# Fused sliding-window attention and leaky-ReLU MLP on one core: the first values loaded as bf16 into their blocks, shared reciprocals, and a new order of the opening

## The chip, the cores and the metric

The kernel runs on one core of a Trainium2 chip. That core has a matrix engine (TensorE, "PE" in the profile; its weight loads are "PEld"), a vector engine (VectorE, "DVE"), a scalar engine (ScalarE, "ACT"), GpSimd ("POOL") and SyncE ("SP"), which here only starts transfers. Each works through its own queue in order. Sixteen DMA engines move data between main memory and on-chip memory; their work comes from SP's queue (plain copies and DMA transposes) and from POOL's queue (copies that also cast fp32 to bf16).

The metric is the device time of one execution in microseconds. Before the change it is 320.06 us, the median of three runs (319.31 to 320.48).

## The reference

Eight batches of eight heads, 576 tokens, head size 64; attention within a window of 32 tokens to either side; then a two-layer MLP over the heads side by side (4608 tokens of 512 values, 2048 hidden).

```python
scores = scale * np.matmul(q, k.transpose(0, 1, 3, 2))
mask = np.abs(pos[:, None] - pos[None, :]) <= 32
scores = np.where(mask, scores, -1000000000.0)
attn = np.exp(scores - max) / (sum + 1e-09)
x = np.matmul(attn, v)            # then heads side by side: 4608 x 512
h = x @ w_in                      # 512 x 2048
g = np.maximum(0.01 * h, h)
out = g @ w_out                   # 2048 x 512
```

All inputs and the output are fp32 in main memory; the kernel computes its matmuls in bf16 with fp32 sums.

## The kernel before, in words

**Tiling.** Two heads make a pair (p = 0..3), and half a batch (288 tokens) is a half. A step of attention is one pair of one half; there are 8 steps to a batch and 64 in all, numbered i = 8·batch + 4·half + pair. Keys and values of a pair lie in block-diagonal tiles (`kbd`, `vbd`, 128x128 blocks of 64 tokens with head a in partitions and columns 64a..64a+63), so that one matmul serves both heads; the off-diagonal parts are zeroed once. A step runs as follows; the letters are those of the opening's list.

- S: five score matmuls into the PSUM tile `ps` (line 322).
- X: the exponential on ACT (line 331). M: the product with the 0/1 window mask on DVE or POOL (line 336), into `prob`.
- B: the sums of each token's exponentials by matmul with `ones_bd`, a 128x128 block of ones for each head, so that each sum comes out in all 64 partitions of its head (lines 363 and 366). R: the reciprocal of these sums on DVE, 128x288 in fp32 (line 374).
- P: five matmuls of `prob` with `vbd` into a PSUM tile (line 396). U: that product times the reciprocal, on DVE, into the bf16 activations `xT` (line 410).

**The MLP.** For each half g there are sixteen H tiles (128 hidden features by 288 tokens, four matmuls over the four pairs, line 424), each followed by E, the leaky ReLU on ACT into `gT` (line 431). An output tile ("o tile") is 128 tokens by 512 and sums sixteen matmuls over the hidden features (line 454), copied out on ACT (line 459) and stored. H tile of half g needs all four steps of half g; the matmul of chunk c needs pair c alone.

**PSUM.** There are eight banks: four turn in the ring `mm` (H tiles, o tiles, transposes, and the sums and products of a few early steps), two hold `ps`, one is `s` (sums) and one is `x` (products).

**The order.** Everything is placed by hand. The first part of the program, batch 0's attention with the first H tiles, is the list `OPENING`: names with the engine that does them. Besides the letters above, zk/zv clear blocks of `kbd`/`vbd`, cq/ck cast q/k of a pair to bf16, tq/tk transpose them on PE, eq and kA/kB copy them from PSUM into place, cv casts one head's values into `vbd`, wi/wo start one quarter of `w_in`/`w_out` (cast by DMA from POOL, 1 MB read and 512 KB written each), f clears the second set of blocks, and `gate` starts the loads of batch 1, which are held back by a one-element memset of the first tile. After the opening a loop runs H tiles 4 to 15 of half 1 and puts the transposes of batch 1's first two pairs between them (`second_pair`). Then a plan of H and o tiles runs: `spend` is called before each group of four o matmuls and each H tile, adds up a planned time, and runs the steps whose due times have passed. There are sixteen such calls (counted from 0 here) in the four o tiles 0 to 3 that lie between half 1's and half 2's H tiles. Steps 8 to 11, half 2, are due at calls 4, 7, 10 and 12; the third and fourth pair of batch 1 are transposed in calls 0 and 3. From batch 2 on q and k are transposed by DMA after casts on POOL, and the later steps follow due times computed from the plan.

**Loads.** q, k and v of batch 0 are loaded in fp32 by SP, except k of pairs 1 to 3, which a DMA from POOL casts (`load_early`, lines 123 to 134). v is loaded one head at a time, 64 tokens by 9 blocks of 64 values (pieces of 256 bytes), and cast into `vbd` by cv on ACT and POOL.

Of the kernel before, what the change touches and what calls it, by code (L numbers as in the profile page):

```python
# [17 lines left out]
    "zk2:ACT zv2:DVE zk3:ACT win:POOL zv1:DVE cq0:DVE zv0:POOL winc:ACT tq0:PE ck0:DVE eq0:ACT mask0:DVE",  # L18
    "zv3:POOL tk0:PE cq1:DVE kA0:ACT tk1:PE mask1:POOL kB0:ACT tq1:PE kA1:DVE S0:PE cq2:ACT eq1:DVE",
    "tk2:PE X0:ACT kB1:DVE cq3:POOL tq2:PE kA2:ACT M0:DVE S1:PE eq2:ACT kB2:DVE B0:PE X1:ACT tq3:PE",  # L20
    "R0:DVE cv00:POOL S2:PE M1:POOL eq3:ACT tk3:PE X2:ACT cv01:POOL kA3:ACT B1:PE M2:DVE wi0:POOL kB3:ACT",
    "P0:PE R1:DVE B2:PE cv11:ACT wi1:POOL S3:PE cv20:ACT cv10:POOL U0:DVE X3:ACT cv21:POOL P1:PE R2:DVE",
    "cv30:ACT S4:PE M3:POOL P2:PE fill4:PE X4:ACT cv31:ACT S5:PE fill3:PE wi2:POOL U2:DVE B3:PE X5:ACT",
    "U1:DVE wi3:POOL P3:PE R3:DVE S7:PE M5:POOL H0c0:PE H0c1:PE H0c2:PE wo0:POOL X7:ACT U3:DVE B5:PE",
    "M4:DVE H0c3:PE f7:POOL R5:DVE P4:PE E0_0:ACT S6:PE E0_1:ACT wo1:POOL P5:PE E0_3:ACT H0_4:PE E0_2:ACT",
    "gate:POOL wo2:POOL E0_4:ACT H0_5:PE U5:DVE X6:ACT B4:PE M7:DVE wo3:POOL H0_6:PE E0_5:ACT R4:DVE",
    "M6:POOL H0_7:PE E0_6:ACT H0_8:PE E0_7:ACT H0_9:PE E0_8:ACT f3:POOL H0_10:PE E0_9:ACT U4:DVE B6:PE",
    "E0_10:ACT f2:POOL P6:PE R6:DVE H0_11:PE H0_12:PE E0_11:ACT f4:POOL H0_13:PE E0_12:ACT H0_14:PE",
    "E0_13:ACT U6:DVE f0:POOL B7:PE E0_14:ACT H0_15:PE R7:DVE f1:POOL P7:PE E0_15:ACT H1c0:PE f6:POOL",
    "H1c1:PE U7:DVE H1c2:PE f5:POOL H1c3:PE",  # L30
]

SPARE_SUMS, SPARE_PRODUCTS = (0, 1, 2), (0, 1, 5)
# [3 lines left out]
def kernel(  # L37
# [14 lines left out]
    nc = tc.nc  # L52
# [35 lines left out]
    def load_qk(b, p, behind=None):  # L88
# [3 lines left out]
        for into, src, name in ((qf, q, "qf"), (kf, k, "kf")):  # L92
            t = fload.tile([96, 2, RUN * D], FP32, name=f"{name}{p}")
            if behind is not None:
                behind.memset(t[0:1, 0, 0:1], 0.0)
                behind = None
# [25 lines left out]

    def load_early():

        for into, src, name, p in ((qf, q, "qf", 0), (kf, k, "kf", 0), (qf, q, "qf", 1), (qf, q, "qf", 2), (qf, q, "qf", 3)):
            t = fload.tile([96, 2, RUN * D], FP32, name=f"{name}{p}")
            nc.sync.dma_start(out=t, in_=src[0, 2 * p:2 * p + 2].rearrange("a (p c) d -> p a (c d)", c=RUN))
            into[0, p] = t
        for p in range(1, NPAIR):
            t = kb[:, p].rearrange("p c a d -> p (c a d)").rearrange("p (a c d) -> p a c d", c=RUN, d=D)  # L130
            nc.gpsimd.dma_start(out=t, in_=k[0, 2 * p:2 * p + 2].rearrange("a (p c) d -> p a c d", c=RUN))
            early[p] = t
        for p in range(NPAIR):
            load_v(0, p)
# [12 lines left out]


# [205 lines left out]
    def sum_mms(i, spare=False):  # L354

        b, hf, p = where(i)
        pr, both, *_ = probs[i]
        if spare:
            s = mmps.tile([128, 512], FP32, name="mm", tag="mm")[:, 0:HALF]
        else:  # L360
            s = xps.tile([128, HALF], FP32, name="s")
        if both is not None:
            nc.tensor.matmul(s, ones_bd, both, start=True, stop=True)  # L363
        else:
            for n in range(2):
                nc.tensor.matmul(
                    s, ones_bd, pr[:, n].rearrange("p c i -> p (c i)"),
# [334 lines left out]
```

## Time and profile before

| what | value |
|---|---|
| three runs | 320.48, 320.06, 319.31 us |
| the profiled execution's own time | 322.44 us |
| its span, first to last instruction | 320.7 us |
| busy PE / DVE / POOL / ACT | 303.8 / 221.3 / 188.2 / 180.7 us |
| reciprocals (line 374), tile from `s` | 61, 1955 ns each |
| first matmul of half 2's H tiles (line 424) | at 63.50 us |

The profile's page shows one execution: busy time by engine, the span in 40 slices, the chain of work that ended last, and groups of like instructions with the mean of one and with what ended the idle time before them. Two more views are used: the timeline of instructions (start, duration, engine, line, output and inputs, count; in brackets the idle time before and what ended it) and the table of windows (busy time per engine in a stretch, then granted clock, DMA share and GB/s). GB/s counts written bytes, so a casting DMA counts half of what it reads.

### The profile page before, as it was taken

How to read it: one execution, taken by the hardware profiler on the slowest of the kernel's cores; microseconds unless marked ns; L12 is line 12 of the kernel's file. 1: busy time of each engine (PE TensorE's matmuls, PEld its weight loads, DVE VectorE, ACT ScalarE, POOL GpSimd, SP SyncE). 2: the span in 40 equal slices, each digit the busy share in tenths (PEclk: the TensorE clock that was granted, in tenths of full speed). 3: DMA queues.
4: the chain of work that ended last, by engine and by line, in shares of the span. 5: the costliest groups of instructions: out<-in, count | busy, mean ns of one | idle time of the engine just before them, and what ended most of it. 6: DMA issues, size and time to landing. Idle time of an engine off the chain costs nothing.

```text
span 320.7 us, 6477 instructions
## 1 busy us (share of the span) xinstructions
PE 303.8 (95%) x2453; PEld 203.6 (63%) x2453; DVE 221.3 (69%) x264; ACT 180.7 (56%) x391; POOL 188.2 (59%) x247
## 2 busy tenths in 40 slices
PE   1889999999999989999999999999999999999995
PEld 0567764585856747676665857676665857576653
DVE  7879556779656969588845988588845988565100
ACT  6866688383734726465552837465552837464531
POOL 8599764965466856486637866586637866330000
PEclk9999999999999999999999999999999999999999
DMA  8989999996999999399834998399833450010101
GB/s 192 192 141 224 268 240 192 250 187 144 219 255 171 255 192 191 73 223 206 186 76 98 214 231 179 73 190 237 187 76 103 106 72 33 34 38 0 65 35 66
DMA packets 108400, 49.01 MB, mean 153 GB/s; under 512 B 68816, under 2 KB 103888, under 8 KB 108368
## 3 DMA queue, kind: packets, MB, share of 16 engines
q1 hardware_dynamic: 103520, 43.96, 65.3%
q0 software_dynamic: 4848, 4.64, 8.9%
q8 instruction: 19, 0.31, 0.4%
q14 instruction: 13, 0.11, 0.1%
HBM read 36.70 MB, written 9.44 MB: 144 GB/s over the span
## 4 chain that ended last, share of the span: by engine, by line
PE 72%; DMA 12%; POOL 8%; DVE 4%; issue 3%; SPq 1%; ACT 1%; DVEq 0%; POOLq 0%; ACTq 0%
PE mm L454 32%; PE mm L424 31%; DMA vf<-in_v_dram 5%; DMA qf<-in_q_dram 5%; PE x L396 4%; PE ps L322 3%; POOL prob L336 2%; DVE r L374 2%; DMA kT<-kb 2%; PE s L363 2%; POOL kb L221 1%; POOL qb L221 1%; DVE kbd L307 1%; POOL w_in_bf L512 1%; POOL vbd L230 1%
## 5 line engine op out<-in xcount | busy, mean ns | idle before, releaser
L374 DVE RECIPROCAL r<-s 128x288 f32<-128x288 f32 x61 | 119.3, 1955 | 54.7 <-PE s L363 51.6
L424 PE MATMUL mm<-xT,w_in_bf 128*128 128x288 bf16 x1024 | 134.0, 286 | 0.6 <-DVE xT L410 0.4
L454 PE MATMUL mm<-w_out_bf,gT 128*128 128x512 bf16 (+2 forms) x592 | 130.4, 374 | 1.1 <-DMA w_out_bf<-in_moe_w_out_dram 1.1
L336 POOL TENSOR_TENSOR prob<-e,mask 128x576 bf16<-128x576 bf16 x60 | 76.4, 1274 | 88.6 <-issue 42.9
L431 ACT ACTIVATE gT<-mm 128x288 bf16<-128x288 f32 x256 | 101.3, 411 | 28.7 <-PE mm L424 12.3
L424 PEld LDWEIGHTS <-w_in_bf 128*128 128x128 bf16 x1024 | 98.2, 98 | 25.5 <-issue 1.2
L454 PEld LDWEIGHTS <-gT 128*128 128x128 bf16 x592 | 56.2, 98 | 60.5 <-issue 1.2
L459 ACT ACTIVATE o_sb<-mm 128x512 f32<-128x512 f32 (+2 forms) x37 | 21.7, 585 | 92.0 <-PE mm L454 92.0
L331 ACT ACTIVATE e<-ps 128x576 bf16<-128x576 f32 x64 | 41.4, 648 | 9.9 <-PE ps L322 8.3
L230 POOL CAST vbd<-vf 64x576 bf16<-64x576 f32 x52 | 36.2, 696 | 1.6
L307 DVE COPY kbd<-kT 64x576 bf16<-64x576 bf16 x48 | 33.2, 691 | 3.2 <-DMA kT<-kb 2.7
L221 POOL CAST kb<-kf 96x384 bf16<-96x384 f32 (+1 forms) x52 | 31.0, 619 | 5.7 <-DMA kf<-in_k_dram 5.7
L410 DVE TENSOR_TENSOR xT<-x,r 128x288 bf16<-128x288 f32 x61 | 27.9, 458 | 7.9 <-PE x L466 1.7
L322 PE MATMUL ps<-qT,kbd 128*128 128x128 bf16 (+2 forms) x320 | 27.3, 219 | 0.0
L322 PEld LDWEIGHTS <-kbd 128*128 128x128 bf16 x320 | 21.5, 102 | 8.5
L396 PE MATMUL x<-prob,vbd 128*128 128x64 bf16 (+1 forms) x305 | 24.8, 213 | 1.5 <-DVE xT L410 0.9
L396 PEld LDWEIGHTS <-vbd 128*128 128x128 bf16 x320 | 20.8, 99 | 8.0 <-issue 3.7
L221 POOL CAST qb<-qf 96x384 bf16<-96x384 f32 x48 | 24.4, 536 | 0.0
L351 DVE TENSOR_TENSOR both<-prob 128x288 bf16<-128x288 bf16 x52 | 20.7, 398 | 1.0 <-POOL prob L336 0.2
L363 PE MATMUL s<-both,ones_bd 128*128 128x288 bf16 x52 | 14.9, 286 | 1.5 <-DVE r L374 1.5
L251 PE MATMUL tp<-ident,qb 96*128 96x96 bf16 x48 | 4.3, 242 | 5.0 <-DVE qb L258 4.9
L228 ACT ACTIVATE vbd<-vf 64x576 bf16<-64x576 f32 x12 | 8.2, 680 | 0.9 <-DMA vf<-in_v_dram 0.6
(60 smaller groups left out, 95.3 us busy)
## 6 DMA issues: line engine op xcount, KB each, us to landing
qf<-in_q_dram SPq DMA_DIRECT2D x32, 288.0 KB, 4.7
vf<-in_v_dram SPq DMA_DIRECT2D x64, 144.0 KB, 4.3
out_dram<-o_sb SPq DMA_DIRECT2D x35, 256.0 KB, 4.0
kf<-in_k_dram SPq DMA_DIRECT2D x29, 288.0 KB, 4.9
w_in_bf<-in_moe_w_in_dram POOLq DMA_DIRECT2D x4, 512.0 KB, 7.8
w_out_bf<-in_moe_w_out_dram POOLq DMA_DIRECT2D x4, 512.0 KB, 17.5
kb<-in_k_dram POOLq DMA_DIRECT2D x3, 144.0 KB, 8.2
qT<-qb SPq DMA_TRANSPOSE x24, 4.1
```

Of the source, the lines that this page charges most:

```text
L221: eng.tensor_copy(out=to, in_=tok)
L230: eng.tensor_copy(out=vbd[b % 2][r, p, :, r], in_=vf[b, p][r])
L307: nc.vector.tensor_copy(out=to.rearrange("p n (m c) -> p n c m", c=2), in_=kT[r].rearrange("p (c n m) -> p n c m", c=2, n=NB),)
L322: nc.tensor.matmul(ps_v[:, n_, :, i0:i0 + n], kbd[b % 2][:, p, blk], by_c[:, :, hf * EVEN + i0:hf * EVEN + i0 + n], start=True, stop=True,)
L331: nc.scalar.activation(out=es[i], in_=ps[:, P0:P0 + 2 * HALF], func=AF.Exp, scale=scale)
L336: eng.tensor_mul(pr.rearrange("p n c i -> p (n c i)"), es.pop(i), mask[hf].rearrange("p n c i -> p (n c i)"),)
L374: nc.vector.reciprocal(r, probs[i][2])
L396: nc.tensor.matmul(x_v[:, :, i0:i0 + n], vbd[b % 2][:, p, blk, :], pr[:, n_, :, i0:i0 + n], start=(blk == parts[0][1]), stop=(blk == parts ...
L410: nc.vector.tensor_mul(place(i), x, r)
L424: nc.tensor.matmul(h[:, 0:HALF], w_in_bf[:, c, ts(f, 128)], xT[:, c, ds(g * HALF % RING, HALF)], start=(c == 0), stop=(c == DMC - 1),)
L431: nc.scalar.activation(out=gT[:, f, ds(g * HALF % RING, HALF)].rearrange("p (i c) -> p i c", c=2), in_=h[:, 0:HALF].rearrange("p (c i) -> ...
L454: nc.tensor.matmul(o[:, lo:hi], gT[:, f, ds(128 * j % RING, 128)], w_out_bf[:, f, lo:hi], start=(f == 0), stop=(f == FFC - 1),)
```

## The change

1. Batch 0's values come as eight DMAs from POOL (`iv0` to `iv7`, one per head) that cast to bf16 and write straight into `vbd`, in pieces of 128 bytes. The eight fp32 loads on SP and the eight casts (cv) are gone. q of pair 3 also comes by a casting DMA from POOL.
2. Steps 0 and 1, and steps 2 and 3, share one reciprocal. B of these steps uses `gather`, which puts each head's sums of a step into 16 rows (two groups of rows per step) of one PSUM tile; one R serves both steps; G, an fp32 matmul with `spread`, spreads a step's reciprocals to 128 partitions in PSUM; C first copies the product of P into fp32 on-chip memory, and U multiplies the two.
3. Only q and k of batch 1's pair 0 are loaded at `gate`, which moves to DVE. The other pairs and all of batch 1's values are loaded after H tile 6 of half 1, held by a one-element activation on ACT.
4. The opening has a new order and new engines for many items; PE starts with 38 filler matmuls (128 columns) and has 11 more between its first transposes, in place of the seven of 224 columns at steps 4 and 5.
5. After the opening: pair 0 of batch 1 is transposed after H tile 10 and the other three in calls 5, 7 and 9 of the o tiles; sums of step 8 and 9 are made ahead in calls 1 and 8; steps 8 to 11 are due at calls 11, 12, 14 and 15.

```diff
 OPENING = [
-    "zk2:ACT zv2:DVE zk3:ACT win:POOL zv1:DVE cq0:DVE zv0:POOL winc:ACT tq0:PE ck0:DVE eq0:ACT mask0:DVE",
-    "zv3:POOL tk0:PE cq1:DVE kA0:ACT tk1:PE mask1:POOL kB0:ACT tq1:PE kA1:DVE S0:PE cq2:ACT eq1:DVE",
-    "tk2:PE X0:ACT kB1:DVE cq3:POOL tq2:PE kA2:ACT M0:DVE S1:PE eq2:ACT kB2:DVE B0:PE X1:ACT tq3:PE",
-    "R0:DVE cv00:POOL S2:PE M1:POOL eq3:ACT tk3:PE X2:ACT cv01:POOL kA3:ACT B1:PE M2:DVE wi0:POOL kB3:ACT",
-    "P0:PE R1:DVE B2:PE cv11:ACT wi1:POOL S3:PE cv20:ACT cv10:POOL U0:DVE X3:ACT cv21:POOL P1:PE R2:DVE",
-    "cv30:ACT S4:PE M3:POOL P2:PE fill4:PE X4:ACT cv31:ACT S5:PE fill3:PE wi2:POOL U2:DVE B3:PE X5:ACT",
-    "U1:DVE wi3:POOL P3:PE R3:DVE S7:PE M5:POOL H0c0:PE H0c1:PE H0c2:PE wo0:POOL X7:ACT U3:DVE B5:PE",
...
+    "fill38:PE zv2:ACT win:POOL zv1:DVE sel:DVE zk3:ACT ld:POOL winc:DVE zv0:DVE cq0:ACT mask0:DVE",
+    "iv0:POOL tq0:PE fill3:PE zk2:DVE ck0:ACT eq0:DVE iv1:POOL tk0:PE fill8:PE zv3:DVE kA0:ACT iv2:POOL",
+    "cq1:DVE kB0:ACT tk1:PE mask1:DVE iv3:POOL tq1:PE kA1:ACT S0:PE cq2:DVE tk2:PE iv4:POOL kB1:ACT",
+    "eq1:DVE tq2:PE iv5:POOL X0:ACT tq3:PE kA2:DVE S1:PE M0:POOL eq2:DVE kB2:ACT tk3:PE X1:ACT eq3:DVE",
+    "iv6:POOL B0:PE kA3:ACT M1:DVE P0:PE S2:PE kB3:ACT iv7:POOL B1:PE C0:DVE R0:DVE X2:ACT wi0:POOL P1:PE",
+    "S3:PE C1:ACT M2:POOL X3:ACT G1:PE M3:DVE wi1:POOL B2:PE B3:PE U1:DVE wi2:POOL S5:PE P3:PE R2:DVE",
+    "P2:PE X5:ACT G0:PE wi3:POOL C2:ACT S7:PE wo0:POOL C3:ACT U0:DVE G2:PE wo1:POOL M5:DVE G3:PE wo2:POOL",
+    "U2:DVE X7:ACT B5:PE H0c0:PE U3:DVE wo3:POOL S4:PE R5:DVE H0c1:PE M7:POOL X4:ACT H0c2:PE H0c3:PE",
+    "S6:PE f7:POOL M4:DVE E0_0:ACT B7:PE P5:PE E0_1:ACT H0_4:PE R7:DVE f0:POOL E0_2:ACT H0_5:PE E0_3:ACT",
+    "H0_6:PE E0_4:ACT f1:POOL P7:PE E0_5:ACT H0_7:PE E0_6:ACT U5:DVE gate:DVE B4:PE X6:ACT f3:POOL",
+    "H0_8:PE U7:DVE P4:PE R4:DVE E0_7:ACT H0_9:PE M6:POOL E0_8:ACT H0_10:PE E0_9:ACT H0_11:PE E0_10:ACT",
+    "H0_12:PE f2:POOL U4:DVE E0_11:ACT B6:PE H0_13:PE E0_12:ACT R6:DVE f4:POOL H0_14:PE E0_13:ACT",
+    "H0_15:PE E0_14:ACT f5:POOL P6:PE E0_15:ACT U6:DVE H1c0:PE f6:POOL H1c1:PE H1c2:PE H1c3:PE",
 ]
-SPARE_SUMS, SPARE_PRODUCTS = (0, 1, 2), (0, 1, 5)
+GROUPS = ((0, 1), (2, 3))
+BANKS = {
+    "B": {0: 'mm', 1: 'mm', 2: 'mm', 3: 'mm', 4: 's', 5: 's', 6: 's', 7: 's'},
+    "P": {0: 'mm', 1: 'mm', 2: 'mm', 3: 'mm', 4: 'x', 5: 'x', 6: 'x', 7: 'mm'},
+    "G": {0: 'mm', 1: 's', 2: 'mm', 3: 'x'},
+}
...
+        elif kind == "ld":
+            load_cast("q", 3)
+            load_cast("k", 3)
+        elif kind == "iv":
+            r = slice(64 * (n % 2), 64 * (n % 2) + 64)
+            nc.gpsimd.dma_start(out=vbd[0][r, n // 2, :, r], in_=v[0, n].rearrange("(c p) d -> p c d", p=64))
...
+        elif kind == "B" and n in group:
+            g = group[n]
+            if g["left"] == len(g["members"]):
+                g["s"] = bank(BANKS["B"][n])[:, 0:HALF]
+            row = 96 - 32 * (n % NPAIR)
+            sums_into(n, g["s"], gather[:, row:row + 128], g["left"] == len(g["members"]), g["left"] == 1)
+            g["left"] -= 1
...
+        elif kind == "G":
+            rows = slice(32 * (n % NPAIR), 32 * (n % NPAIR) + 32)
+            probs[n][2] = bank(BANKS["G"][n])[:, 0:HALF]
+            nc.tensor.matmul(
+                probs[n][2], spread[rows].rearrange("p h x -> p (h x)"), group[n]["r"][rows], start=True, stop=True,
+            )
...
+        elif kind == "C":
+            x = attn.tile([128, HALF], FP32, name="x_sb", bufs=4)
+            copy(eng, x, probs[n][3])
+            probs[n][3] = x
...
         elif kind == "gate":
-            load_next(eng)
+            load_qk(1, 0, eng)
...
     cast_qk(1, 0, nc.vector)
-    cast_qk(1, 1, nc.vector)
...
-        if f in (7, 11):
-            second_pair((f - 7) // 4)
...
+        if f == 6:
+            for p in range(1, NPAIR):
+                load_qk(1, p, nc.scalar if p == 1 else None)
+            for p in range(NPAIR):
+                load_v(1, p)
+        if f == 10:
+            second_pair(0)
...
-    due = [O_US * n for n in (4, 7, 10, 12)]
+    due = [O_US * n for n in (11, 12, 14, 15)]
...
-        if turn == 1:
-            second_pair(2)
         if turn == 2:
+            sums(8)
+            cast_qk(1, 1, nc.vector)
+        if turn in (6, 8, 10):
+            p = turn // 2 - 2
+            second_pair(p)
+            if p < 3:
+                cast_qk(1, p + 1, nc.vector)
+        if turn == 7:
             score(9)
-        if turn == 4:
-            second_pair(3)
+        if turn == 9:
+            sums(9)
+        if turn == 10:
             cast_v(1, 0, nc.scalar)
```

## The prediction

> **What bounds the kernel now.** I read the page's slices, then the chain of waits, the timeline at PE's waits, the landing times, and the windows of 2 us.
>
> ```profile
> PE   1889999999999989999999999999999999999995
> DMA  8989999996999999399834998399833450010101
> ```
>
> A slice is 8 us. From the ninth on PE is full, and there both programs have the same instructions at the same planned places. So the time moves by what the first H matmul of half 2 moves (63.50 us now), unless a later stage gives it back.
>
> ```profile
> 2.74 9.24 DMA qf<-in_q_dram
> 25.43 0.08 POOL qf L95
> 25.53 6.11 DMA qf<-in_q_dram
> 31.66 17.22 DMA vf<-in_v_dram
> 48.96 0.68 ACT vbd L228
> ```
>
> This is the chain: up to 49 us it runs through loads, and through POOL, which issues the weights and then the gate.
>
> ```profile
> 5.25 2.40 DVE L258 CAST kb<-kf 96x768 bf16<-96x768 f32 x1 [0.41 <-DMA kf<-in_k_dram]
> 16.79 0.66 PE L322 MATMUL ps<-qT,kbd 128*128 128x96 bf16 x5
> 22.13 0.40 PE L322 MATMUL ps<-qT,kbd 128*128 128x64 bf16 x5
> 35.42 0.65 PE L424 MATMUL mm<-xT,w_in_bf 128*128 128x288 bf16 x4 [0.36 <-DVE xT L410]
> 48.45 1.02 PE L454 MATMUL mm<-w_out_bf,gT 128*128 128x512 bf16 x4 [1.06 <-DMA w_out_bf<-in_moe_w_out_dram]
> 57.72 0.95 POOL L221 CAST kb<-kf 96x384 bf16<-96x384 f32 x2 [0.29 <-DMA kf<-in_k_dram]
> 63.50 0.78 PE L424 MATMUL mm<-xT,w_in_bf 128*128 128x288 bf16 x5
> ```
>
> From the timeline: the five matmuls of S take 0.66 us until 20 us and 0.40 after, though the granted clock reads 1.00 throughout. Half 1 (35.42) waits for the last U of batch 0. The first o tile waits for the last quarter of `w_out` (48.45). POOL waits for batch 2's k (57.72).
>
> ```profile
> w_in_bf<-in_moe_w_in_dram POOLq DMA_DIRECT2D x1, 512.0 KB, 5.5
> w_out_bf<-in_moe_w_out_dram POOLq DMA_DIRECT2D x1, 512.0 KB, 12.7
> w_out_bf<-in_moe_w_out_dram POOLq DMA_DIRECT2D x1, 512.0 KB, 22.2
> ```
>
> First and last quarter of the weights: issued at 15.8, 22.9 (first of `w_out`) and 26.2, they land at 21.3, 35.6 and 48.4. All eight land at 21.3, 24.6, 27.7, 30.8, 35.6, 40.3, 44.8 and 48.4: 3.1 us apart almost alone, 4.5 beside batch 1's loads.
>
> ```profile
> 12.00:14.00 2.00, 1.95 (x19) 1.11 (x19) 1.94 (x3) 1.51 (x4) 1.94 (x3) 1.00 1.09 178
> 16.00:18.00 2.00, 1.45 (x12) 1.00 (x11) 2.00 (x3) 1.82 (x3) 1.96 (x3) 1.00 0.21 22
> 40.00:42.00 2.00, 2.00 (x26) 1.68 (x24) 1.40 (x3) 1.93 (x6) 0.00 (x0) 1.00 1.16 267
> 50.00:52.00 2.00, 1.60 (x12) 0.89 (x13) 1.95 (x1) 1.93 (x4) 0.00 (x0) 1.00 0.63 142
> ```
>
> The last two columns are DMA share and GB/s. DMA has holes at 16 to 18 and 50 to 52 us; values alone (12 to 14) move 178 GB/s.
>
> **The change part by part: the opening.** Removed: two of eight reciprocals (1.95 us each) from DVE, which sets the pace from 13 to 35 us; eight v casts (0.66 to 0.97) from POOL and ACT; the fp32 cast of k pair 0 on DVE (2.40, beside POOL's memsets; 0.5 to 0.55 for the same shape elsewhere), now 0.84 on ACT. Added on DVE: three small memsets, a reduction and a small copy (0.1 to 0.2 each), beside the wait for the first load: nothing on the path. Added on POOL: eight v issues and one q issue at 0.64 to 0.83 (k and weight rows).
>
> Step by step, with these durations. DVE clears, copies masks and `win` until 6.9, eq0 to 7.6; ACT kA0, kB0 to 8.6; S0 at 8.7 (was 9.8). ACT does kA1 and kB1 before X0: M0 ends on POOL at 12.0, M1 on DVE at 13.7 (12.15 and 14.8 before). P0 needs values 0 and 1, issued at 6 to 7.4; with k's 7 us to landing they come at 13 to 14. C0 then holds DVE to 14.2, R(0,1) to 16.15, M3, U1, R(2,3) 17.45 to 19.4, U0, M5, U2, U3 to 21.3 (U3 was 24.6). H0c0 waits until U2 frees its fourth `mm` bank. R5, M4, R7, U5, the gate, U7, R4, U4, R6, U6 follow to 31.8 (the last U was 35.4). Half 1's third chunk starts there; before, only the fourth waited, at 35.42. One more chunk of four matmuls (0.5) is left: 3.1 us gained.
>
> Waits added. The program gives POOL's DMAs eight semaphores in turn, so iv4 waits for the first k, and each weight issue for a value (wi0 for iv0, wo3 for iv7). M2 and M7 stand behind them on POOL. If values land by 17 us these cost nothing; U0 and U2 give 1.4 us of slack. P0 stands before S2 on PE.
>
> G is a fp32 matmul; no row shows one. Ends: 0.13 (bf16, 288 columns) and 1.3 (four times the slow 0.33). I take 0.5, near their geometric middle; it is on the path twice. The FP8 and Floating Point Precision page of the Trainium skill (TensorE Precision Notes) says four passes, which would make 0.5 too. C costs 0.41 on ACT (line 431's shape), off the path, and 0.45 on DVE for C0, counted. The fillers end near 5.6 (38 at 0.11 to 0.15, the transposes' pace) while PE waits for q anyway. If they do not speed PE up, four matmul groups on the path cost 0.25 more each: 1 us; if they do, nothing is left to add. I take the fast pace: it appeared right behind the old fillers of 19.4 to 21.3.
>
> **The weights.** Values now run ahead of the weights on POOL's queue without the hole of 16 to 18 us. All eight take 6.6 us at 178 GB/s from about 9, so the first quarter streams from 16 (17.5 now, 1.7 after its issue): 1.7 us gained. Quarters 1 to 5 follow at 3.1; pair 0 of batch 1 (0.59 MB, gated at 26) costs 1.2. The rest of batch 1 waits for ACT's seventh E of half 1, 36 us, so only the last quarter runs at 4.5 rather than four of them. `w_out` is complete at 43.9 (21.3 − 1.7 = 19.6, then 6 × 3.1 + 1.2 + 4.5), or 42.5 if that quarter keeps 3.1 too: loads issued at 25.5 slowed the quarter of 35.6, not that of 30.8. I take 43.4, against 48.4. PE gets to that quarter at 42.3: 31.9 + 8 H matmuls 1.0 + 12 tiles × 0.49 + transposes, S8 and B8 1.0 + 12 o matmuls 2.6.
>
> **From there to half 2.** Now 48.45 to 63.50, 15.05. After: 52 o matmuls × 0.216 = 11.2; three pairs of transposes 1.4 (none now); S9 to S13, B9 to B11, P8 to P11 at 0.25 each, 3.0; together 15.6. Steps 10 and 11 now lie one call (0.86) apart: B11 needs the `s` bank that R10 holds (1.95), P11 the `x` bank until U10 (0.46), and R11 and U11 come after; PE waits 0.65 + 0.2 + 0.9 = 1.75. So half 2 starts at 43.4 + 15.6 + 1.75 = 60.75.
>
> **Batch 2's k** is a second path: its landing, the cast 0.95, M12 1.27, the joining add 0.58, R11 1.96, U11 0.46, some 5.3 in all with gaps; DVE has the add in front of R11. The bytes ahead of it are the same. Holes worth 3.1 us of full DMA (1.65 at 16 to 18, 1.45 at 50 to 54) may close; I take 2.0, as SP still has only eight loads in flight. Landing 57.7 + 0.95 (end of the cast 58.67) less 2.0 leaves U11 at 61.0; the six H matmuls ahead of the fourth chunk (0.75) make this a start of 60.3.
>
> **The sum.** The later path sets the start, 60.75 against 63.50: −2.75 us. The profiled execution took 322.44 (span 320.7), so 319.7 is its sum; it stands 2.4 above the median of the runs, and the same difference off the median of 320.06 gives 317.3.
>
> **The rivals.**
>
> 1. *Values come slowly in pieces of 128 bytes* (slower). No row has such writes; 256-byte pieces run at 178 GB/s, larger ones at 267. At half the 178, values take 13 us instead of 6.6: the weights move by 6.5, `w_out` to 49.9, half 2 to 67.25, 323.8. It decides from 2.75 us of lateness, values taking over 9.4. For it: smaller pieces are slower in the rows. Against: the casting DMAs of k landed with the plain ones. The Trainium skill, DMA: Bandwidth & Descriptors (Specifications), says that below 512 bytes a transfer falls under line rate by read-modify-write; both old and new pieces are below, and the trace agrees for 256.
>
> 2. *DVE and POOL hold each other up* (no change). The 2.40 us cast beside POOL's memset shows it. DVE's on-chip copies and clears from 5.9 to 13.6 are two masks 1.7, two clears 1.1, two casts 1.0: 3.8. If POOL's issues waited for all, the weights would move by as much: 43.4 + 3.8 + 17.35 = 64.55, +1.05: 321.1. Against: k's issues took 0.63 to 0.83 beside DVE's clears at 1.6 to 3.6. The Trainium skill, SBUF — State Buffer (two separate sides), has a rule for it: descriptors of POOL's DMAs wait while DVE holds the shared port.
>
> 3. *DMA has no less to do* (no change). k of batch 2 lands at 57.7 as before, holes only moved; then half 2 starts at 63: 319.7.
>
> 4. *Batch 1 behind the weights is late* (slower). Beside weights its loads ran at 0.295 MB in 2.06 us; ten of this size, from 37, would end at 57.6, P11 and R11 behind them; half 2 at 65: 321.7. Against: weights end near 43, and then 240 GB/s apply (53 us).
>
> 5. *DMA stays full* (faster still). All 3.1 us of holes close and PE's later stalls on line 374 (1.5 us, at 100 to 150 us) fall away: 315.
>
> **How the numbers follow.** Forecast 0.42; rival 5 0.15; rivals 2 and 3 0.21; rival 1 0.15; rival 4 0.07. Faster by over 0.5% (1.6 us, about what three runs within 1.2 us can tell) 0.57, within 0.5% 0.21, slower 0.22. The forecast's own range is 315.9 to 318.4. For 8 in 10: 314.0 leaves 0.05 below, 322.5 leaves most of rival 1 above, 0.13.
>
> **What would show it.** Right: last U of batch 0 near 31.8, the four o matmuls behind `w_out`'s last quarter near 43.4, half 2 near 60.8, a wait of line R's tile before step 11's B and P, DMA share above 1 from 10 to 18 us. Wrong: values landing after 18.4; POOL waiting between iv4 and wi3; PE idle over 1 us between 33 and 60 for batch 1's loads; PE's S at 0.66 after 8 us.

## The result and the profile after

The changed kernel takes 329.97 us (median of four runs, 328.93 to 332.53) against 320.00 for the kernel before: ratio 1.0325, 95% interval 1.0258 to 1.0392. It is slower by 10 us where I forecast 2.75 us less, and lies outside my range. The profiled execution took 330.79 us, with a span of 329.1 (before: 322.44 and 320.7). The ratios in this document leave out three executions, one each of e6, e7 and e11, that took over 1.5% more than the fastest of their kernel, and are not ratios of the medians.

The page's slices of 8 us:

```profile
PE   7799987859999999999999999999999999999995
PEclk9958999987999999999999999999999999999999
DMA  8999899947996779459942899379823631010101
```

New is the 5 in the clock's third slice, with a 7 in the tenth. DMA is full earlier than before; the 4 is a hole that the windows of 2 us place at 38 to 40 us.

The windows of 2 us (PE, PEld, DVE, ACT, POOL busy, then clock, DMA share, GB/s):

```profile
14.00:16.00 2.00, 0.64 (x6) 0.56 (x7) 1.91 (x2) 1.57 (x3) 1.61 (x3) 1.00 1.11 72
16.00:18.00 2.00, 2.00 (x17) 1.45 (x17) 1.46 (x3) 0.20 (x1) 2.00 (x3) 0.71 1.18 186
22.00:24.00 2.00, 2.00 (x14) 1.39 (x12) 2.00 (x3) 0.27 (x1) 2.00 (x3) 0.50 1.24 206
26.00:28.00 2.00, 2.00 (x20) 1.61 (x19) 0.61 (x1) 1.21 (x4) 0.49 (x1) 0.73 1.27 214
38.00:40.00 2.00, 2.00 (x18) 1.61 (x17) 0.00 (x0) 1.75 (x7) 0.82 (x1) 1.00 0.21 34
72.00:74.00 2.00, 1.62 (x9) 1.06 (x9) 0.55 (x2) 0.71 (x2) 1.36 (x3) 0.50 0.60 129
```

From about 16.8 to 27.1 us TensorE is granted half its clock, right when PE has become full; again from 71.4 to 78.3, behind a wait of 3.07 us. In the chain of waits (start, duration) the two stretches are seen as H matmuls at half pace:

```profile
23.69 2.88 PE mm L439 x12
...
36.85 3.60 PE mm L439 x28
...
75.13 4.54 PE mm L439 x24
80.27 3.43 PE mm L439 x28
```

Twelve took 2.88 us, where 28 take 3.43 to 3.60 at full clock; the 24 at 75.13 took 2.94 in the kernel before.

What PE waited for between 44 and 78 us, changed kernel first (us in total, times, longest), then the kernel before:

```profile
PE mm L439 <- DVE xT L425: 3.1, 1, 3.1
PE ps L347 <- ACT e L356: 1.4, 3, 0.8
PE ps L347 <- DVE kbd L330: 1.2, 1, 1.2
PE tp L276 <- DVE qb L246: 0.6, 1, 0.6
```

```profile
PE mm L454 <- DMA w_out_bf<-in_moe_w_out_dram: 1.1, 1, 1.1
PE x L396 <- ACT vbd L228: 0.4, 1, 0.4
```

The whole list of the changed kernel sums to 7.1 us, that of the kernel before to 1.5. The largest is the fourth chunk of half 2's first H tiles, which waits for the last U of step 11: it starts at 72.38 us, against 64.24 (63.50 and six matmuls), so 8.1 us are lost ahead of it. From there to the end it is 256.7 us now and 256.5 before, but that these agree is chance. In the profiles of e10 (the kernel before with fillers) and e13 (the changed kernel with its clock held) the same stretch takes 253.8. The kernel before has 2.1 us of waits there, at 119 to 125 us, which e10's profile has not; the changed kernel has its second stretch at half clock. Against the median of the kernel before, the profiled execution is 10.8 us longer, about what 8.1 ahead of this chunk and 2.9 behind it make. The timeline of ACT in these steps:

```profile
57.97 2.79 ACT L253 ACTIVATE vbd<-vf 64x576 bf16<-64x576 f32 x4
60.79 0.65 ACT L356 ACTIVATE e<-ps 128x576 bf16<-128x576 f32 x1
61.33 0.59 ACT L474 ACTIVATE o_sb<-mm 128x512 f32<-128x512 f32 x1
61.95 1.39 ACT L253 ACTIVATE vbd<-vf 64x576 bf16<-64x576 f32 x2
63.36 0.65 ACT L356 ACTIVATE e<-ps 128x576 bf16<-128x576 f32 x1
64.03 1.39 ACT L253 ACTIVATE vbd<-vf 64x576 bf16<-64x576 f32 x2
65.45 0.65 ACT L356 ACTIVATE e<-ps 128x576 bf16<-128x576 f32 x1
```

Each of these exps (`e`) stands behind two or four casts of values of 0.70 us. The five matmuls of step 10's score began on PE at 58.68 and took 0.40; its exp began at 60.79. The order is not new: in the kernel before, too, ACT does the casts ahead of the exps (casts at 50.99, 53.08 and 55.66, exps at 52.41, 54.49 and 57.07). New is how little else PE has to do between the scores of steps 10 to 13: 4, 8 and 4 o matmuls, and 12, 12 and 8 in the kernel before. POOL and DVE carry it on, ending with the U that PE waits for:

```profile
65.31 0.95 POOL L246 CAST qb<-qf 96x384 bf16<-96x384 f32 x2
66.20 0.95 POOL L246 CAST kb<-kf 96x384 bf16<-96x384 f32 x2
67.12 1.27 POOL L361 TENSOR_TENSOR prob<-e,mask 128x576 bf16<-128x576 bf16 x1
```

```profile
68.42 1.47 DVE L376 TENSOR_TENSOR both<-prob 128x288 bf16<-128x288 bf16 x1 [1.16 <-POOL prob L361]
69.82 1.95 DVE L395 RECIPROCAL r<-s 128x288 f32<-128x288 f32 x1
71.87 0.46 DVE L425 TENSOR_TENSOR xT<-x,r 128x288 bf16<-128x288 f32 x1
```

M12 waits behind batch 2's casts, the joining add waits for M12, and R11 stands behind that add on DVE. These queues, too, have the same order in the kernel before, where the last U falls under the sixteen o matmuls ahead of half 2:

```profile
60.05 3.62 PE L454 MATMUL mm<-w_out_bf,gT 128*128 128x512 bf16 x16
62.49 0.46 DVE L410 TENSOR_TENSOR xT<-x,r 128x288 bf16<-128x288 f32 x1
```

From P11 to the end of U11 it is 3.1 us there (59.81 to 62.95) and 5.0 here (67.32 to 72.33). Between P11 and the fourth chunk PE has sixteen o matmuls there and four here, 2.6 us less. So of the wait of 3.1 us some 1.3 come from the cover that is gone, and 1.9 from the longer chain.

Batch 0's values and the weights came in time (DMA issues; last number, median us to landing):

```profile
w_in_bf<-in_moe_w_in_dram POOLq DMA_DIRECT2D x4, 512.0 KB, 7.4
w_out_bf<-in_moe_w_out_dram POOLq DMA_DIRECT2D x4, 512.0 KB, 16.1
vbd<-in_v_dram POOLq DMA_DIRECT2D x8, 72.0 KB, 4.7
```

### The profile page after: what moved, and what is told of

Its sections match the earlier page's. It is cut to its first block, busy times and chain, and to the rows that moved or that the text cites. A ratio compares the mean times of both kernels' runs of the same rounds, so it can differ in the third digit from the quotient of the medians.

```text
span 329.1 us, 6567 instructions
## 1 busy us (share of the span) xinstructions
PE 312.0 (95%) x2489; PEld 209.7 (64%) x2509; DVE 216.6 (66%) x274; ACT 180.0 (55%) x390; POOL 184.9 (56%) x244
## 4 chain that ended last, share of the span: by engine, by line
PE 86%; DVE 3%; ACT 3%; DMA 2%; issue 2%; POOL 2%; SPq 0%; DVEq 0%; ACTq 0%; POOLq 0%
PE mm L439 38%; PE mm L469 35%; PE ps L347 5%; PE x L411 4%; PE s L389 3%; DMA qf<-in_q_dram 2%; POOL prob L361 1%; DVE r L395 1%; PE mm L599 1%; ACT vbd L253 1%; DVE kbd L330 1%; ACT kT L301 1%; ACT qT L281 1%; ACT e L356 1%; DVE both L376 0%
## 5 line engine op out<-in xcount | busy, mean ns | idle before, releaser
L395 DVE RECIPROCAL r<-s 128x288 f32<-128x288 f32 x60 | 117.4, 1957 | 63.2 <-PE s L389 63.1
L439 PE MATMUL mm<-xT,w_in_bf 128*128 128x288 bf16 x1024 | 138.3, 291 | 3.2 <-DVE xT L425 3.1
L439 PEld LDWEIGHTS <-w_in_bf 128*128 128x128 bf16 x1024 | 100.2, 100 | 29.9 <-issue 3.6
L255 POOL CAST vbd<-vf 64x576 bf16<-64x576 f32 x48 | 33.1, 690 | 1.4
L425 DVE TENSOR_TENSOR xT<-x,r 128x288 bf16<-128x288 f32 x59 | 27.0, 457 | 8.5 <-PE x L411 2.7
L332 DVE COPY kbd<-kT 64x576 bf16<-64x576 bf16 x48 | 32.3, 674 | 0.3
L411 PE MATMUL x<-prob,vbd 128*128 128x64 bf16 (+1 forms) x295 | 24.0, 213 | 0.5 <-ACT vbd L253 0.3
L330 DVE COPY kbd<-kT 64x576 bf16<-64x576 bf16 x8 | 3.5, 442 | 10.2 <-ACT kT L301 10.2
L389 PEld LDWEIGHTS <-ones_bd 128*128 128x128 bf16 x68 | 6.6, 100 | 2.4 <-issue 1.5
```

Of the source, the lines that this page charges most:

```text
L255: eng.tensor_copy(out=vbd[b % 2][r, p, :, r], in_=vf[b, p][r])
L332: nc.vector.tensor_copy(out=to.rearrange("p n (m c) -> p n c m", c=2), in_=kT[r].rearrange("p (c n m) -> p n c m", c=2, n=NB),)
L389: nc.tensor.matmul(s, lhs, part, start=start and n == 0, stop=stop and n == len(parts) - 1, skip_group_check=True,)
L395: nc.vector.reciprocal(r, s)
L411: nc.tensor.matmul(x_v[:, :, i0:i0 + n], vbd[b % 2][:, p, blk, :], pr[:, n_, :, i0:i0 + n], start=(blk == parts[0][1]), stop=(blk == parts ...
L439: nc.tensor.matmul(h[:, 0:HALF], w_in_bf[:, c, ts(f, 128)], xT[:, c, ds(g * HALF % RING, HALF)], start=(c == 0), stop=(c == DMC - 1),)
```

## The experiments

Two causes are to be told apart: the order of batch 1's steps (parts 3 and 5 of the change) and the granted clock. A third, the late loads, is a rival within the first. All sixteen results first, with their names shortened; "clock" is the mean granted clock of the executions, lowest to highest. Of each kernel's ratio, the base is the kernel before on the same chip (319.7 to 320.5).

| kernel | median us | ratio, 95% interval | clock |
|---|---|---|---|
| changed | 329.97 | 1.0325 [1.0258, 1.0392] | 0.964–0.979 |
| e1 fillers | 327.91 | 1.0212 [1.0159, 1.0265] | 0.984–0.995 |
| e2 rest as before | 321.21 | 1.0015 [0.9988, 1.0042] | 0.973–1.0 |
| e3 both | 321.90 | 1.0049 [1.0018, 1.0080] | 0.982–0.995 |
| e4 rest alone | 328.76 | 1.0255 [1.0207, 1.0302] | 0.995–1.0 |
| e5 spread | 324.15 | 1.0127 [1.0070, 1.0184] | 0.973–0.988 |
| e6 three earlier | 325.17 | 1.0140 [1.0098, 1.0182] | 0.972–1.0 |
| e7 loads at gate | 329.45 | 1.0241 [1.0166, 1.0316] | 0.969–1.0 |
| e8 no fillers | 329.71 | 1.0266 [1.0212, 1.0320] | 0.984–0.995 |
| e9 casts behind | 323.74 | 1.0127 [1.0075, 1.0178] | 0.984–1.0 |
| e10 before, warmed | 319.81 | 0.9994 [0.9968, 1.0020] | 0.978–1.0 |
| e11 new order | 319.89 | 0.9987 [0.9955, 1.0019] | 0.973–0.999 |
| e12 new order, fillers | 318.24 | 0.9944 [0.9913, 0.9975] | 0.989–1.0 |
| e13 dense fillers | 324.89 | 1.0163 [1.0110, 1.0215] | 0.99–1.0 |
| e14 casts, fillers | 324.55 | 1.0130 [1.0085, 1.0175] | 0.989–1.0 |
| e15 before, new order | 322.05 | 1.0087 [1.0057, 1.0117] | 0.995–1.0 |
| e16 changed again | 328.39 | 1.0254 [1.0205, 1.0303] | 0.974–0.984 |

### Which part: e1 to e4

e1 adds 28 fillers of 128 columns to the opening, into a bank that is free:

```diff
- ... tk3:PE X1:ACT ... wi0:POOL P1:PE S3:PE C1:ACT ...
+ ... tk3:PE hold6:PE X1:ACT ... wi0:POOL P1:PE hold11:PE S3:PE hold11:PE C1:ACT ...
```

> The changed kernel with 28 more filler matmuls (128 columns, into the sums' bank that is free there): 6 after the transposes of k pair 3, 11 after product 1, 11 after the scores of step 3. They fill the stretch from 14 to 16 us, where PE was busy 0.64 of 2 us before its granted clock fell to 0.50 (16.6 to 27 us). Theory 'clock': the clock stays at 1.00, the last U of batch 0 comes at 31.5 us instead of 35.1, and the time falls by 3.5 to 5 us, to 325 to 326.5. Theory 'crowded steps' (steps 8 to 11 at calls 11 to 15 set the start of half 2, whatever the opening does): the opening gets faster but the wait before half 2 takes it up; 328.5 to 330.

e2 keeps the changed opening and puts back parts 3 and 5 (loads of batch 1 together at the gate, transposes and due times as before):

```diff
-    due = [O_US * n for n in (11, 12, 14, 15)]
+    due = [O_US * n for n in (4, 7, 10, 12)]
-            load_qk(1, 0, eng)
+            for p in range(NPAIR):
+                load_qk(1, p, eng if p == 0 else None)
+            for p in range(NPAIR):
+                load_v(1, p)
```

> The changed kernel with what follows the opening as in the kernel before: all loads of batch 1 at the gate, pairs transposed after H tiles 7 and 11 and in calls 0 and 3, no sums ahead, steps 8 to 11 at calls 4, 7, 10, 12. Theory 'crowded steps': no wait before half 2's fourth chunk, half 2 starts near 65 us with the clock still halved from 16 to 27; 322 to 324. Theory 'clock': the rest was not the cause; 327 to 330, little changed.

e3 is e1 and e2 together.

> Both edits: the fillers that hold the clock, and the rest as in the kernel before. If the two causes are separate and add up, half 2 starts at 61 to 62 us and the time is 317.5 to 319.5, faster than the kernel before. If a third cause in the new opening remains (weights, the values' transfers, the fp32 spread), it stays above 321.

e4 is the kernel before with parts 3 and 5 alone.

> The kernel before with only the part behind the opening changed: pair 0's loads alone at the gate, the others after H tile 6 of half 1, pairs transposed after H tile 10 and in calls 5, 7, 9, sums 8 and 9 ahead, steps 8 to 11 at calls 11, 12, 14, 15. Theory 'crowded steps': half 2 waits some 4 to 6 us as in the changed kernel, PE idles long enough for the clock to fall, 325 to 328. Theory 'clock': within 1 us of the kernel before, 319 to 321.

Parts 3 and 5 alone make the kernel before slower by 2.55% (9.0 us between the medians), with the clock at 0.995 or more: the order costs by itself. Taking them out of the changed kernel (e2) brings it level with the kernel before. PE's longest waits in e4 from 44 to 78 us are those of the changed kernel: 3.1 us for U, 1.4 for exps, 1.2 for `kbd`. The clock is the smaller term: e1 gained 2 us. e3 gained nothing over e2: its fillers did not hold the clock, which in the profiles of both was at 0.50 for 6.8 us (from 9.0 in e2, from 10.4 in e3).

In e2 the changed opening gains nothing. PE comes to batch 1 earlier and then waits for the casts of its k (3.4 us in e3); their loads share the DMAs with the weights:

```profile
PE tp L276 <- POOL kb L246: 2.9, 2, 1.7
```

### Where in the order: e5 to e7, e9

e5: only the due times and, for that, the first v casts move.

```diff
-    due = [O_US * n for n in (11, 12, 14, 15)]
+    due = [O_US * n for n in (9, 11, 13, 15)]
-        if turn == 10:
+        if turn == 8:
             cast_v(1, 0, nc.scalar)
```

> The changed kernel with steps 8 to 11 due at calls 9, 11, 13, 15 instead of 11, 12, 14, 15, and the casts of values 0 and 1 of batch 1 two calls earlier; the last step keeps its call. Crowding theory (two steps in a row put four v casts of 0.70 us ahead of two exps on ACT, and two reciprocals of 1.96 behind each other on DVE): the waits of S for ACT's exps (2.1 us in four) fall under 0.8, R11 starts within 0.5 us of B11, and the wait in front of half 2's fourth chunk falls from 3.1 to about 1; the time falls by 3 to 4 us, to about 326. Rival (the last step is simply due too near to half 2): the wait of 3.1 stays, time 328 to 330. Rival (batch 1's loads, issued 10 us later, decide): PE waits for casts of k or v appear as the steps come earlier, time unchanged at 329 to 330.

e6: the block as a whole, in the same bunching, three calls earlier.

```diff
-    due = [O_US * n for n in (11, 12, 14, 15)]
+    due = [O_US * n for n in (8, 9, 11, 12)]
-        if turn in (6, 8, 10):
+        if turn in (3, 5, 7):
...
```

> The changed kernel with the whole block of batch 1 (transposes of pairs 1 to 3, S9, B9, the first v casts, steps 8 to 11) three calls (2.6 us of o matmuls) earlier, in the same bunching: due at 8, 9, 11, 12, transposes at the ends of calls 2, 4, 6. If the nearness of the last step to half 2 is what costs, the wait of 3.1 us in front of half 2's fourth chunk goes and the waits for ACT's exps stay near 2: about 326.5. If the crowding itself decides, PE loses the same 2 us among calls 8 to 12 and the tail wait is gone as well, since three calls of o matmuls lie behind it: also 326 to 327, so only the place of the waits differs here from the run with the steps spread. If the late loads decide, PE waits for POOL's casts of k (1 to 3 us) and for v casts take the place of the tail wait: 328.5 to 330.

e7: all of batch 1's loads at the gate, the order as changed.

```diff
-            load_qk(1, 0, eng)
+            for p in range(NPAIR):
+                load_qk(1, p, eng if p == 0 else None)
+            for p in range(NPAIR):
+                load_v(1, p)
-        if f == 6:
-            ...
```

> The changed kernel with all of batch 1 issued at its gate on DVE (29.6 us) instead of only pair 0 there and the rest behind ACT's eviction at 38.8. Crowding theory: nothing of the order changes, so steps 8 to 11 stand where they stood and the time stays within 1 us of the changed kernel: 328.5 to 330.5. Rival (late loads decide): the waits of 3.1 and 2.1 us shrink, and the time falls to 323 to 325. The hole in DMA at 38 to 40 us (share 0.21) is filled in either case.

e9: the v casts behind the step instead of ahead of it.

```diff
+            step()
             if i < 11:
                 cast_v(1, i - 7, nc.scalar)
-            step()
```

> The changed kernel with one thing moved: the two v casts of each following pair (0.70 us each) are issued behind a step's exp instead of ahead of it on ACT. Dues, loads and transposes as in the changed kernel. If ACT's queue is what stretches steps 8 to 11, the waits of S for ACT's exps (1.4 to 2.1 us) fall under 0.4, S13 and B11 come about 1.5 us earlier, and the time falls by 1 to 2 us, to 328 to 329. If the stretch comes from DVE and POOL (two reciprocals in a row, M12 behind POOL's casts, the joining add of 1.47 us), the wait in front of half 2's fourth chunk grows by what the exps give back, and the time stays within 0.7 us of the changed kernel's 330.

Late loads are not the cause: e7's profile has the rest of batch 1 issued from 27.3 us, that of the changed kernel from 39.0, and e7 measured as the changed kernel, with the same wait of 3.1 us for U and a new one of 1.8 us for `w_out`, which now shared the DMAs:

```profile
PE mm L439 <- DVE xT L425: 3.1, 1, 3.1
PE mm L469 <- DMA w_out_bf<-in_moe_w_out_dram: 1.8, 1, 1.8
```

Spreading the steps (e5) and moving them away from half 2 (e6) both help, and PE's waits from 44 to 78 us sum to 4.4 and 4.6 us for 7.1. In e5 no score waits for an exp any more, though waits for `kbd` grow from 1.2 to 3.2; in e6 the wait for exps stays (1.6 us) and that for the last U is 0.4. So both are real: the steps were too near to each other and to half 2. It is not the clock alone: e6's one execution at a clock of 1.00 took 322.25, and the three at 1.00 of the changed order (e13 below) 324.06 to 324.99. e9 changes nothing but ACT's order, and its timeline shows the exp between the casts:

```profile
56.43 0.65 ACT L356 ACTIVATE e<-ps 128x576 bf16<-128x576 f32 x1
57.11 1.39 ACT L253 ACTIVATE vbd<-vf 64x576 bf16<-64x576 f32 x2
58.52 0.60 ACT L474 ACTIVATE o_sb<-mm 128x512 f32<-128x512 f32 x1
59.01 0.65 ACT L356 ACTIVATE e<-ps 128x576 bf16<-128x576 f32 x1
```

Its wait for U falls to 2.3 us and that for exps is gone; waits sum to 5.6. That is 1.5 us, and yet the time fell by 6.2 against the first executions of the changed kernel, and by 4.7 against those on the same chip (e16). I had expected 1 to 2. The rest is the clock, as the last runs show.

### The clock: e8, e10, e13, e14, e16

e8 takes the 49 fillers out; e10 puts 38 of them ahead of the kernel before and changes nothing else.

```diff
-    "fill38:PE zv2:ACT win:POOL ...
+    "zv2:ACT win:POOL ...
```

> The changed kernel without its 49 small filler matmuls at the start (38, 3 and 8). Theory of the clock (an early busy stretch followed by a stretch where PE idles costs the granted clock): the clock column reads 1.00 from 6 to 40 us, the matmul groups take the slow pace (0.57 to 0.66 for an S) until about 18 to 22 us, and the twelve H matmuls that took 3.09 us at 23.5 take 1.6; last U of batch 0 near 32 to 33.5 instead of 35.1; time down by 1.5 to 3 us, to about 327. Rival (the fillers are what keeps the opening short, the drop comes from elsewhere): the drop to 0.50 stays somewhere between 10 and 28 us, S and P are slower before it, and the time is 330 or more.

```diff
-    "zk2:ACT zv2:DVE ...
+    "warm38:PE zk2:ACT zv2:DVE ...
```

> The kernel before with 38 small filler matmuls ahead of everything on PE and nothing else. Theory (a warm clock that is lost again costs as much as it gave): S groups take 0.40 instead of 0.65 us from 9 us on, then in most executions a stretch of 8 to 10 us at a granted clock near 0.50 appears between 8 and 30 us, the mean clock falls from 0.998 to about 0.98, and the time is 320 to 322. Rival (warming early is a plain gain): clock column 1.00 throughout, the last U of batch 0 0.5 to 1 us earlier, time 319 to 320 or a little less.

In e8 the stretch at 0.50 stayed (18 to 28 us) and the time too: it does not need the fillers, and that theory fell. e8's mean clock is higher (0.984 to 0.995), but its first three scores, at 10.0 to 14.5 us, took 0.60 to 0.65 us with the column at 1.00, where the changed kernel's took 0.40. In e10 a stretch shows where the clock column of the kernel before shows none, right behind a window in which PE had nothing:

```profile
6.00:8.00 2.00, 0.00 (x0) 0.00 (x0) 1.59 (x3) 1.97 (x4) 2.00 (x3) 0.97 1.14 251
8.00:10.00 2.00, 1.71 (x23) 1.35 (x23) 1.56 (x3) 0.52 (x2) 0.84 (x2) 0.50 1.22 240
12.00:14.00 2.00, 2.00 (x26) 1.57 (x25) 1.97 (x2) 1.78 (x4) 1.89 (x3) 0.50 1.21 197
```

The time is level. Half 1's fourth chunk, which waits for batch 0's last U, starts at 35.40 us, and at 35.42 in the kernel before: neither the warm start nor the stretch got through to it.

e13 adds to e1's 28 fillers another 14 where PE waits for the k of pair 1, and leaves the order as changed; e14 adds e9's move; e16 is the changed kernel once more on that chip.

```diff
- ... tk0:PE fill8:PE zv3:DVE ... tk3:PE X1:ACT ... wi0:POOL P1:PE S3:PE C1:ACT ...
+ ... tk0:PE fill22:PE zv3:DVE ... tk3:PE hold6:PE X1:ACT ... wi0:POOL P1:PE hold11:PE S3:PE hold11:PE C1:ACT ...
```

> The changed kernel with the 42 fillers of the last run in the opening and nothing else: the clock held (mean 0.99 or more), the order of batch 1 unchanged. If the clock costs 3.5 to 4 us of the 10 and the order 6, the time is 325.5 to 326.5, with the wait in front of half 2's fourth chunk still at 3 us. If the clock were the main cause: 321 to 323. If the 50-percent stretch only moves behind the 3 us wait at 69 us: 328.

> The same fillers and the v casts behind the exps, all else as in the changed kernel. If the casts' place on ACT is worth 2.5 to 3.5 us by itself at an equal clock: 322.5 to 323.5. If it was worth all of the 6 us that its run gained: 320. If that gain came from the clock: 325 to 326, as without the move.

> The changed kernel once more, beside the others on one chip: 328 to 332 us, mean clock 0.96 to 0.985, and among its executions 1.4 to 1.7 us more for each 0.01 of clock lost.

With the clock at 1.00 in three of four executions, e13 takes 324.89 us, 3.5 under e16's 328.39 on the same chip: the clock's part. It still is 5.2 us above the kernel before (319.71), with the waits of the changed kernel in it (6.8 us of the 7.1; timeline of PE):

```profile
65.44 0.90 PE L439 MATMUL mm<-xT,w_in_bf 128*128 128x288 bf16 x6
69.43 0.77 PE L439 MATMUL mm<-xT,w_in_bf 128*128 128x288 bf16 x5 [3.09 <-DVE xT L425]
```

e14 did not give the 322.5 to 323.5 that I expected: 324.55, not to be told from e13. Its one execution at clock 1.00 took 322.85, e9's took 323.40, e13's three 324.06 to 324.99; so the casts' place is worth 1 to 2 us at an equal clock, by one execution each. The rest of e9's gain goes with a better clock (0.984 to 1.0, for 0.964 to 0.984 in the changed kernel), which its edit was not meant to touch.

Among executions of one kernel the time mostly follows the clock: e7 took 326.40 at 1.00, 327.95 at 0.984 and 330.96 at 0.969; e6 322.25 at 1.00 and 326.90 at 0.972; e16 326.72 at 0.984 and 329.32 at 0.974; e2 319.24 at 1.00 and 321.89 at 0.973. That is 1.0 to 2.6 us for each 0.01. It is no law: two executions of e8, both at 0.995, took 327.02 and 330.46.

### A version faster than both: e11, e12, e15

e11 takes the changed opening, issues the rest of batch 1 behind ACT's fifth eviction of half 1, casts and transposes pairs 1 to 3 earlier, spreads the steps and puts the v casts behind them. e12 adds e13's fillers. e15 gives this order to the kernel before.

```diff
-    due = [O_US * n for n in (11, 12, 14, 15)]
+    due = [O_US * n for n in (8, 10, 11, 13)]
-        if f == 6:
+        if f == 4:
-        if turn in (6, 8, 10):
-            ...
+        if turn == 3:
+            second_pair(1)
+            cast_qk(1, 3, nc.vector)
+        if turn in (5, 7):
+            second_pair((turn - 1) // 2)
+        ...
```

> The changed kernel's opening with a new order of batch 1: rest of the loads behind ACT's fifth eviction of half 1 instead of its seventh (about 1 us earlier), casts of pairs 1 to 3 at calls 0, 1, 2, transposes at the ends of calls 2, 4, 6, S9 at call 5, B9 at call 7, steps 8 to 11 at calls 8, 10, 11, 13, and the v casts behind the step's exp on ACT. Crowding theory: waits of PE between 44 us and half 2 sum to under 2 us (4.4 with the dues spread alone), the wait in front of half 2's fourth chunk under 0.7, half 2's first matmul at 62 to 63 in an execution whose clock stays at 1.00; the time 318 to 320 with the clock at 1.00 and 320 to 322 with one stretch at 0.50: median near 320.5, level with the kernel before. Rival (the transfers set the pace whatever the order): waits for casts of k and v of 2 to 4 us, time 323 to 325.

> The same new order with 42 more filler matmuls in PE's waits between 6.5 and 16 us (14 more ahead of the third k, then 6, 11 and 11). Theory (the stretch at 0.50 follows windows in which PE is little used): fewer and shorter stretches, mean clock 0.99 or more in most executions, time 1 to 2 us under the run without them: 318.5 to 320. Rival (the fillers are too few, or the reaction does not go by this): the stretch is there as often, and the fillers, at half pace where it falls on them, cost 0.5 to 1 us.

> The kernel before with its own opening and loads of pair 0 at its gate, and batch 1 in the new order (loads behind ACT's fifth eviction of half 1, steps at calls 8, 10, 11, 13, v casts behind the exps). If the changed opening is worth the 1.5 to 2 us by which its last U comes earlier, this is at 319.5 to 321, level with the kernel before and 1.5 to 2 above the faster version. If the new order alone made the faster version: 318.

e12 takes 318.24 us, 0.9944 of the kernel before [0.9913, 0.9975], a small gain, but its interval leaves out 1. In its timeline half 2 starts without a wait, 1.9 us earlier than in the kernel before (63.50); the second line is e15's:

```profile
61.62 1.83 PE L439 MATMUL mm<-xT,w_in_bf 128*128 128x288 bf16 x12
62.91 1.63 PE L427 MATMUL mm<-xT,w_in_bf 128*128 128x288 bf16 x12
```

e11, without the fillers, is level with the kernel before. e15 is 3.8 us slower than e12, and slower than the kernel before. But its half 2 starts 0.6 us earlier than in the kernel before and only 1.3 later than in e12, so the changed opening, with its clock held, is worth 1.3 us, and the new order the other 0.6 of e12's 1.9. The rest of e15's loss lies behind the start of half 2. From the fourth chunk to the end its profile takes 256.4 us and not 253.8, with PE waiting for DVE's reciprocals and for U at 72 to 83 us; there DVE's copies of keys into `kbd`, two at a time, take 1.92 and 2.09 us, against 1.04 and 1.33 in e10 at the same place. The kernel before's profile has such waits at 119 to 125 us. e12's has them at 72 to 78 us, and its execution of 320.62 us is the slowest of e12's ten. What sets them off was not tested.

## Why the prediction was wrong

**The opening's sum was nearly right, the pace under it was not.** S0 came at 8.89 us (8.7 forecast). The last U of batch 0, forecast at 31.8, began at 35.07 in the changed kernel and at 32.1 in e13. One step that failed is "if they do, nothing is left to add. I take the fast pace": I priced the fillers by whether PE would become fast, never by whether it would stay so. The clock fell in the new opening, with fillers at its start or without them (e8), and that cost 3.5 us (e16 against e13). Even at a held clock the gain is smaller than the 3.1 us that I forecast, for PE reached half 1's first chunk only at 31.55 us in e13, with all four chunks of its first tiles left and not two. The first o matmul comes 2.55 us earlier than before, and 1.0 of this is two pairs of transposes that moved behind it.

**G** took 0.75 us at full clock where it was on the path (L599, x2), and not 0.5: 0.25 too little, and I had it on the path twice. The four-pass reading of the FP8 and Floating Point Precision page of the Trainium skill (TensorE Precision Notes) gave 0.5 as well. Both left out what a matmul that stands alone takes beyond its columns: one of 288 columns in bf16 takes 0.29 us in e13's trace, where in a row they follow each other at 0.12. Four times 0.12 and the other 0.17 would make 0.65, an estimate from these rows.

**The values and weights** were right or better: values landed 4.7 us after their issue (median), the last near 16 us, ahead of the weights. The first quarter of the weights landed at 19.9 (19.6 forecast), `w_out` complete near 40 (43.4). So rival 1 is out, in spite of small pieces: at 14 to 16 us the window shows 72 GB/s at a DMA share of 1.11, counted in bf16. Rival 2 is out: the value issues took 0.73 to 0.76 us each beside DVE's work. Rival 3 and the hole: I had batch 1 issued at 36 and the weights ending at 43; the loads came later (39.0) and the weights ended earlier, and DMA stood at 0.21 from 38 to 40 us.

**The tail is the main error.** The step that failed is "PE waits 0.65 + 0.2 + 0.9 = 1.75". It should have been near 7: the waits after 44 us sum to 7.1 in the trace, 6.8 in e13 at full clock. I followed the two banks `s` and `x`, and nothing of the queues that I had named for others: on ACT four and then two casts of 0.70 us ahead of each exp (1.4 us of PE's waiting, and all of the chain's later steps with it); on POOL batch 2's casts ahead of M12 (1.8 us, 1.0 of it after M12's exp was done); on DVE the joining add, 0.58 in the kernel before and 1.47 here beside POOL's cast, ahead of R11. The last step was due one call ahead of half 2, 0.86 us, where the chain from P11 to U11 took 5.0. The kernel before had four calls of o matmuls (16, from 60.05 to 63.50) behind its last step, which hid its 3.1 us at no price; I costed the later due times at the bank waits alone and did not name that cover. Of the links, the runs tested the casts on ACT (e9, e14: 1 to 2 us) and the distances (e5, e6); what POOL's casts and DVE's add cost is read from the timelines alone.

**Batch 2's k** as a second path: I put U11 on it at 61.0; the casts and M12 are on it, but it began with a late exp, not with a landing.

**Rival 4** looked in the right place for the wrong reason: in e7 the loads are earlier and the waits for U, exps and `kbd` are the same. No rival of mine said that the order of ACT's queue would hold half 2, and the 0.22 that I gave to "slower" rested mostly on rival 1. Rival 5's last part looks as if it came true: PE's waits beyond 80 us, 2.1 us in the profile of the kernel before, are not in that of the changed one. But they are not in e10's either, whose program is the same there, so they belong to that one execution and are no gain of the change.

The account at one clock, from the timelines of PE (the kernel before, then e13): the first o matmul comes at 41.30 us in e13, 2.55 ahead of the 43.85 of the kernel before.

```profile
43.85 1.03 PE L454 MATMUL mm<-w_out_bf,gT 128*128 128x512 bf16 x4
41.30 1.03 PE L469 MATMUL mm<-w_out_bf,gT 128*128 128x512 bf16 x3
```

From there to half 2's fourth chunk it is 28.1 us (to 69.43) against 20.4 (to 64.24): 7.7 lost, of which waits over 0.2 us make 5.6 (7.1 against 1.5) and two more pairs of transposes 1.0; the rest are shorter pauses. Net 5.2, as measured between the medians. The clock's 3.5 is the difference of e16's and e13's medians, so with it the sum is e16's 8.7 by itself (328.39 against 319.71); in the profiles of these two the fourth chunk lies 4.3 us apart (73.77 and 69.43). The first four executions of the changed kernel, at lower clocks, showed 10.

## What to carry to other kernels

When steps are moved later, write down, engine by engine, what stands ahead of each link of the chain that the next stage waits for, and how much work still covers the last link; a bank's release is only one of these links. Put casts that a later step needs behind the exp that the present one needs. A saving in an opening is worth what the clock lets it be: look at PE's busy share in each window behind a warm-up, and compare executions at equal clock before believing that an edit gained. Look, too, whether the one execution that was profiled is like the median of its kernel, before two profiles are subtracted.

## What the runs showed of the hardware

**Half clock while PE is full.** The stretch lasted from 16.8 to 27.1 us in the changed kernel's profile and longer in another execution (e16, windows):

```profile
10.00:12.00 2.00, 1.77 (x33) 1.46 (x34) 2.00 (x4) 1.50 (x3) 1.43 (x2) 0.63 2.24 154
16.00:18.00 2.00, 0.93 (x2) 0.50 (x2) 1.32 (x2) 0.63 (x1) 2.00 (x3) 0.50 1.07 166
18.00:20.00 2.00, 2.00 (x14) 1.32 (x14) 0.95 (x2) 0.00 (x0) 2.00 (x4) 0.50 1.19 190
26.00:28.00 2.00, 2.00 (x12) 1.32 (x11) 1.08 (x2) 0.67 (x2) 2.00 (x3) 0.60 1.21 179
```

**The stretches come in whole lengths of 3.4 us.** The share of a window at 0.50 gives its edges: 0.71 from 16 to 18 is 1.16 us at 0.50, 0.73 from 26 to 28 is 1.08, so the changed kernel's first stretch is 1.16 + 8 + 1.08 = 10.2 us. In the same way e16's is 17.1 (1.48 + 14 + 1.6), the changed kernel's second 6.8 (0.56 + 6 + 0.28), e10's 6.8, and each of the two in e14's profile 3.4: five, three, two and one times 3.4. The mean clocks of the changed kernel's executions (e16's with them) fit this: 0.984, 0.979, 0.974 and 0.964 are three, four, five and seven such lengths at half clock in 327 to 331 us. One length can cost PE at most half of it, 1.7 us.

The Trainium skill, TensorE: Matmul & The Clock Gate (HAM oscillation — how this bites in real kernels), sets the rule that PE should not idle for more than about 3.4 us. Here the longest gaps ahead of the drop in the changed kernel's profile were 0.72 and 0.69 us, with PE busy for 0.64 of 2 us; so the clock can fall without such a gap. The same page of the Trainium skill (Part 1) has the full clock back after one busy window of 3.4 us; in the trace PE was full for 10 us at 0.50 before it came back. What exactly sets it off stays open: e6's profile has PE busy for 0.62 of 2 us in the same place and the clock at 1.00 throughout:

```profile
14.00:16.00 2.00, 0.62 (x10) 0.37 (x7) 1.96 (x1) 1.79 (x4) 1.54 (x2) 1.00 1.15 68
```

Nor does the wait of 3.1 us for U always bring a stretch: one follows it in the changed kernel's profile, and none in those of e1, e4, e7, e8, e13 and e16, which have the same wait of 3.07 to 3.09 us. It differs between executions of one kernel. Fillers that keep PE above 1.8 of 2 us in most windows from 6 to 18 us (e12, e13) kept the mean clock at 0.989 or more in all 18 executions (with e14), which makes the stretches fewer but does not rule them out: e14's profile has two.

**A reading to beware of:** in the kernel before the clock column reads 1.00 from the start, while a score takes 0.66 us until 20 us and 0.40 after. The column did not show that first slow stretch; the durations did.
